# A two-layer interleaved attention kernel on one NeuronCore: the scheduler's planned times for DMA issue and landing, cross-engine waits, layer norm and softmax are changed

## The chip, the cores and the metric

One core of a Trainium2 chip runs the kernel. The metric is device time in microseconds (us), the median of the runs. Five engines work side by side, each through its own list of instructions in order: TensorE (PE, with its weight loads shown apart as PEld), VectorE (DVE), ScalarE (ACT), GpSimd (POOL) and SyncE (SP). SP issues the DMAs spoken of here. An instruction that has to wait holds back everything behind it on its engine.

## The reference

Four residual layers work on 2048 positions of width 576. Layers 1 and 3 ("A") are a dilated local attention; layers 2 and 4 ("B") are a recurrent attention over 64 segments of 32 positions, where each segment also sees 8 memory rows that the segment before left.

```python
def _A_ref(x, wqkv, wo):                   # H = 32 heads of 18, W = 8 keys, every 2nd position
    qkv = (x @ wqkv) ...                   # [3, H, S, 18]
    kg, vg = k[:, :, idx_c], v[:, :, idx_c]          # keys pos, pos-2, .. pos-14
    attn = softmax(where(mask, q . kg * 18 ** -0.5, -1e9))
    return (attn . vg) @ wo

def _B_ref(x, mem0, Wq, Wk, Wv, Wo, seg_len):        # 32 heads of 128
    mem = mem0                                       # 8 rows
    for s in range(n_seg):
        h = concatenate([mem, x[s * 32:(s + 1) * 32]])
        q, k, v = h Wq, h Wk, h Wv
        p = softmax(where(mask, q k^T * 128 ** -0.5, -1e9))
        o = (p v) Wo
        mem, out_s = o[:8], o[8:]

x = x + _A_ref(_layernorm(x), A_wqkv, A_wo)
x = x + _B_ref(_layernorm(x), B_mem0, ...)
x = x + _A_ref(_layernorm(x), A_wqkv, A_wo)
x = x + _B_ref(_layernorm(x), B_mem0, ...)
```

## The kernel before

The program runs 70 steps. In step t, `b_step` takes segment t of layer 2 and segment t-6 of layer 4 together: 80 columns in the tile `hT`, of which 16 are memory. It does the query and key products (`qk`, eleven groups of three heads, L728 and L730), the value products (`vpass`, L759), the scores with a softmax (`scores`, `softmax`), the products with the values (`pv_m` for the memory rows, L817; `pv_x` for the others, L850), and the output projection (`oproj`, L874). The memory rows of the output go straight into the next step's `hT`.

Every second step a tile of 64 positions of layer 1 and one of layer 3 (`a_tile`) go through beside this: load, layer norm, the three projections (L479), the key products on POOL, the logits on PE (L528), a softmax, the probabilities spread back over rows by PE in two parts (L552: 16 matmuls, then 4), the products with the values on DVE, a tree of three additions (tile `big`, then `oT`), the output projection (L587), and a second layer norm whose result goes out to HBM as `xn2T` or `xn4T`. From there `load_x` fetches it into a step's `hT` (L704).

The weights of the A layers do not stay on the chip's inner memory. They lie in HBM as 20 blocks, and each tile fetches all 20 again, one DMA per block (`wblock`, L423), into a ring of six buffers named `ring`. That makes 1280 loads. A block's five matmuls free its buffer for the next load.

PE writes into PSUM. Three tiles `r` there serve nearly everything (`qk`, `vpass`, `scores`, the layer norms' sums, the projections). One large tile `o` (pool `o4`) serves the spreading and both products with the values in turn. The next writer of such a tile waits until ACT or DVE has carried the last contents out.

What sets the order is a planner. Each piece of work is an operation with an engine, a planned length `us`, a priority, the operations it depends on and the buffers it takes (`_Plan.op`). `_Plan.run` plays the program with those lengths: when an engine comes free it takes the ready operation with the lowest priority number whose buffers are free, and at that moment the operation's instructions are written into the engine's list. A result counts as there `LAT` after the operation's end, or `lat` where that is given. Where an operation may run on either of two engines, the one that is free first in the plan takes it. So a planned time changes no instruction; it changes the order in which each engine gets them, and which of two engines gets some. On the chip the real waits are held by semaphores.

```python
                        if all(len(self.pools[p]) >= k for p, k in need.items()):
                            pick = o
                            break
...
                    heapq.heappush(events, (free[e] + (self.LAT[e] if o.lat is None else o.lat), n, ("done", o)))
```

Of the kernel before, what the change touches and what calls it, by code (L numbers as in the profile page):

```python
# [10 lines left out]
ACT = mybir.ActivationFunctionType  # L11
# [14 lines left out]
D = 576  # L26
T = 64
NS = T // SEG
# [27 lines left out]
class _Plan:  # L56
# [2 lines left out]

    LAT = {"PE": 0.22, "DVE": 0.1, "ACT": 0.1, "POOL": 0.12, "SP": 2.4, "NONE": 0.0}
    SWITCH = 0.1

    def __init__(self):
# [129 lines left out]
class _K:  # L195
# [190 lines left out]
    def layernorm(self, xT, dep, prio, writer, wus, wacq=(), wuses=()):  # L386

        nc, pl = self.nc, self.pl
        xs, st, ps = pl.buf("xs"), pl.buf("st"), pl.buf("r")
        a = pl.op(AD_, (0.46, 0.49), lambda e: self.copy(e, xs.t[:, :, 0, :], xT.t[:]), prio, [dep], acq=[xs], uses=[xT])  # L390

        def square(e):
            if e == "ACT":
                nc.scalar.activation(out=xs.t[:, :, 1, :], in_=xT.t[:], func=ACT.Square)
# [9 lines left out]
        c = pl.op("PE", 0.29, mm, prio, [b], acq=[ps], uses=[xs])  # L404

        def stats(e):
            m, r = st.t[:, 0, :], st.t[:, 1, :]
            nc.vector.tensor_scalar(out=m, in0=ps.t[:, 0:T], scalar1=1.0 / D, scalar2=None, op0=ALU.mult)
            nc.vector.tensor_tensor(out=r, in0=m, in1=m, op=ALU.mult)
            nc.vector.scalar_tensor_tensor(out=r, in0=ps.t[:, T:2 * T], scalar=1.0 / D, in1=r, op0=ALU.mult, op1=ALU.subtract)  # L410
        d = pl.op("DVE", 0.8, stats, prio, [c], acq=[st], uses=[ps])

        def rstd(e):
            r = st.t[:, 1, :]
            nc.scalar.activation(out=r, in_=r, func=ACT.Ln, bias=self.epsb[:, 0:1], scale=1.0)
            nc.scalar.activation(out=r, in_=r, func=ACT.Exp, scale=-0.5)
        f = pl.op("ACT", 0.6, rstd, prio, [d], uses=[st])
        return pl.op("POOL", wus, lambda e: writer(e, st.t[:, 0, :], st.t[:, 1, :]), prio, [f], acq=wacq,
                     uses=[st, xT, *wuses])

    def wblock(self, i, prio, dep):
        w = self.pl.buf("ring")
        o = self.pl.op("SP", 0.4, lambda e: self.nc.sync.dma_start(out=w.t[:], in_=self.wA[i]), prio, [dep], acq=[w], lat=2.7)  # L423
        return w, o

    def a_tile(self, layer, j, dep, due, span):
# [4 lines left out]
        def pr(f):  # L431
            return due - span * (1.0 - f)
        xT = pl.buf("xT")
        if layer == 1:
            x0, ps = pl.buf("x0"), pl.buf("r")
            a = pl.op("SP", 0.4, lambda e: nc.sync.dma_start(out=x0.t[0:T, 0:D], in_=self.A_x[0, j * T:(j + 1) * T, :]),
                      pr(0), [dep], acq=[x0])

            def tr(e, ps=ps):
# [6 lines left out]
        else:  # L446
            dl = pl.buf("dl")

            def ld(e):
                nc.sync.dma_start(out=xT.t[:], in_=self.x1T[:, j])  # L450
                nc.sync.dma_start(out=dl.t[:], in_=self.dT[0][:, NS * j:NS * j + NS])
            a = pl.op("SP", 0.8, ld, pr(0), [dep, self.x1_stored[j], *self.d_stored[0][NS * j:NS * j + NS]], acq=[xT, dl])

            def add(e):
                xv = xT.t[:].rearrange("p c (s n) -> p c s n", n=SEG)
# [111 lines left out]
                   pr(0.6), [b], uses=[ps, big])  # L567
        mus = []
        for c0, nb in ((0, 2), (2, 2), (4, 1)):
            mus.append(pl.op("DVE", 0.15 + 0.27 * nb,  # L570
                             lambda e, c0=c0, nb=nb: self.tt(e, big.t[:, c0:c0 + nb], big.t[:, c0:c0 + nb], win(vT.t, c0, nb), ALU.mult),
                             pr(0.62), evs + [got[2], got[2, "h"]] if nb == 2 else [e4, got[2], got[2, "h"]], uses=[big, vT]))
        oT = pl.buf("oT")
# [19 lines left out]
        xst = pl.op("SP", 0.4, lambda e: nc.sync.dma_start(out=(self.x1T if layer == 1 else self.x3T)[:, j], in_=xT.t[:]),  # L593
                    pr(0.95), [o], uses=[xT])
        (self.x1_stored if layer == 1 else self.x3_stored)[j] = xst
        xnb = pl.buf("xnb")
# [1 line left out]
        def wr2(e, m, rstd):  # L598
# [12 lines left out]
        o = pl.op("SP", 0.4, lambda e: nc.sync.dma_start(out=self.xnT[lane][:, NS * j:NS * j + NS], in_=xnb.t[:]),  # L611
                  pr(0.95), [o], uses=[xnb])
        self.xn_stored[lane][j] = o

    def finish_out(self, j, prio):
# [6 lines left out]
        a = pl.op("SP", 0.8, ld, prio, [self.x3_stored[j], *self.d_stored[1][NS * j:NS * j + NS]], acq=[xT, dl])  # L622
# [6 lines left out]
        for n, (c0, c1) in enumerate(((0, 4), (4, 5))):  # L629
# [8 lines left out]
            def ev(e, n=n, ps=ps):  # L638
# [6 lines left out]
        pl.op("SP", 0.4, lambda e: nc.sync.dma_start(out=self.out[0, j * T:(j + 1) * T, :], in_=ot.t[0:T, :]), prio, [o],  # L645
              uses=[ot])


# [6 lines left out]
    def softmax(self, ps, e_, n, prio, dep, mul, view, eview, last, pt, ptpool):  # L655
# [20 lines left out]
        def norm(e):  # L676
# [4 lines left out]
            nc.vector.reciprocal(out=s, in_=s)  # L681
            if mul == "DVE":
                nc.vector.tensor_tensor(out=v, in0=v, in1=s.unsqueeze(len(shp) - 1).to_broadcast(shp), op=ALU.mult)
# [11 lines left out]
    def load_x(self, t):  # L695

        nc, pl = self.nc, self.pl
        hT = pl.buf("hT")
        self.hT[t] = hT
        segs = [(l, self.lane_seg(t, l)) for l in range(2) if self.lane_seg(t, l) is not None]  # L700

        def ld(e):
            for l, s in segs:
                nc.sync.dma_start(out=hT.t[:, :, XC[l]:XC[l] + SEG], in_=self.xnT[l][:, s])  # L704
        o = pl.op("SP", 0.4 * len(segs), ld, t - 0.42, [self.xn_stored[l][s // NS] for l, s in segs] + [self.qk_op.get(t - 1)],
                  acq=[hT])
# [192 lines left out]
    def x_out(self, t, dep, prio):  # L899
# [8 lines left out]
        for lane in range(2):  # L908
            s = self.lane_seg(t, lane)
            if s is not None:  # L910
                self.d_stored[lane][s] = pl.op("SP", 0.4, lambda e, lane=lane, s=s: nc.sync.dma_start(out=self.dT[lane][:, s], in_=st.t[:, lane]),
                                               prio, [o], uses=[st])

    def b_step(self, t):
# [123 lines left out]
```

## Time and profile before

| what | value |
|---|---|
| median of 3 runs | 2835.91 us (2834.46 to 2848.84) |
| profiled execution, its own time | 2859.22 us |
| span of that execution | 2857.4 us |
| PE busy | 2451.8 us, 86% |
| DVE, ACT, POOL busy | 1839.1, 977.9 and 882.5 us |
| mean granted TensorE clock | 0.960 |
| DMA moved | 304.10 MB, mean 106 GB/s |

The profile page gives busy times, a chain of work that ended last, and groups of instructions. The view of waits lists who waited for whom: total us, number of times, the longest. The view of windows gives each engine's busy time in chosen stretches with the granted clock. The timeline lists instructions in order of time; its number in brackets is the engine's idle time just before, with what ended it. The profiled execution took 23.3 us more than the median of the runs; one sum below is made against the profiled time and then carried over.

### The profile page before, as it was taken

To read this page: it belongs to the slowest core of one execution; us is meant where nothing else is said; L and a number is where in the kernel's file an instruction comes from. 1 tells how busy PE (TensorE), PEld (TensorE's weight loads), DVE (VectorE), ACT (ScalarE), POOL (GpSimd) and SP (SyncE) were. 2 spreads that over 40 slices of the span, in tenths; PEclk is the share of its full clock that TensorE was granted. 3 is DMA by queue.
4 is the path that set the end of the run, shared out by engine and by line. 5 is a ranking of instruction groups with operands and counts; after the bars stand their busy time and mean duration, and the time that the engine had idled before them with its cause. 6 is when DMAs were issued, how large, how long until landed. Compare 5 with 4: busy or idle time off the path is not lost.

```text
span 2857.4 us, 159357 instructions
## 1 busy us (share of the span) xinstructions
PE 2451.8 (86%) x73360; PEld 2021.4 (71%) x73360; DVE 1839.1 (64%) x3981; ACT 977.9 (34%) x2165; POOL 882.5 (31%) x1122
## 2 busy tenths in 40 slices
PE   0289999888898998888898989889889898999998
PEld 0177777777777776777777777777777777777777
DVE  1266777666666676666766667666666666766665
ACT  0023333333333333333433333333333333332222
POOL 3321333233333333323333333333333333321110
PEclk9999999999999999999999999999999999999999
DMA  7622344333434434333434433433343443332210
GB/s 264 185 60 71 102 111 121 100 95 105 113 112 121 115 99 115 103 91 105 119 109 118 122 107 105 117 107 94 105 114 109 118 121 110 100 87 74 79 34 18
DMA packets 368644, 304.10 MB, mean 106 GB/s; under 512 B 146788, under 2 KB 364452, under 8 KB 366436
## 3 DMA queue, kind: packets, MB, share of 16 engines
q1 hardware_dynamic: 364724, 275.02, 34.5%
q0 software_dynamic: 3248, 18.88, 1.8%
q8 instruction: 573, 9.39, 1.4%
q14 instruction: 99, 0.81, 0.1%
HBM read 260.88 MB, written 32.90 MB: 103 GB/s over the span
## 4 chain that ended last, share of the span: by engine, by line
PE 58%; DVE 15%; DMA 10%; ACT 9%; issue 4%; SPq 3%; POOL 1%; ACTq 0%; DVEq 0%; POOLq 0%
PE r L728 17%; PE psY L874 14%; PE r L759 12%; DMA ring<-wA_blk 10%; PE r L479 5%; PE r L730 4%; DVE big L230 4%; ACT big L223 3%; DVE big L225 2%; SPq L300 2%; DVE OT L225 2%; ACT OT L223 2%; PE o L817 2%; PE o L850 1%; DVE r L671 1%
## 5 line engine op out<-in xcount | busy, mean ns | idle before, releaser
L728 PE MATMUL r<-hT,wq 128*128 128x80 bf16 x8960 | 695.0, 202 | 31.3 <-DVE V L225 17.3
L728 PE MATMUL r<-hT,wk 128*128 128x80 bf16 x8960 | 694.1, 202 | 0.0
L728 PEld LDWEIGHTS <-wq 128*128 128x128 bf16 x8960 | 468.1, 100 | 86.5 <-issue 79.3
L759 PE MATMUL r<-wv,hT 128*32 128x512 bf16 x6720 | 481.2, 408 | 12.9 <-ACT em L673 3.4
L874 PE MATMUL psY<-OT,wo 128*128 128x80 bf16 (+1 forms) x11360 | 474.7, 210 | 17.4 <-issue 9.3
L225 DVE CAST qk<-r 128x480 bf16<-128x480 f32 (+1 forms) x465 | 294.1, 632 | 299.3 <-PE r L730 295.1
L874 PEld LDWEIGHTS <-wo 128*128 128x128 bf16 x11360 | 457.3, 105 | 23.7 <-issue 22.1
L728 PEld LDWEIGHTS <-wk 128*128 128x128 bf16 x8960 | 465.4, 100 | 0.0
L730 PE MATMUL r<-hT,wq_r 128*128 128x80 bf16 x2240 | 452.6, 202 | 1.8 <-issue 1.8
L730 PE MATMUL r<-hT,wk_r 128*128 128x80 bf16 x2240 | 452.9, 202 | 0.0
L230 POOL TENSOR_TENSOR big<-qT,kT 128x1024 bf16<-128x1024 bf16 (+1 forms) x192 | 329.0, 1722 | 152.6 <-ACT kT L223 143.9
L759 PEld LDWEIGHTS <-hT 128*32 128x32 bf16 x8400 | 214.9, 101 | 224.8 <-issue 77.3
L479 PE MATMUL r<-xn,ring 128*128 128x64 bf16 x4800 | 236.2, 198 | 99.1 <-DMA ring<-wA_blk 83.1
L230 POOL TENSOR_TENSOR ex<-ex,sum 128x384 bf16<-128x384 bf16 x140 | 124.1, 886 | 603.8 <-DVE sum L681 383.0
L479 PEld LDWEIGHTS <-ring 128*128 128x128 bf16 x4800 | 179.0, 100 | 162.4 <-DMA ring<-wA_blk 108.9
L223 ACT ACTIVATE qk<-r 128x480 bf16<-128x480 f32 x305 | 170.4, 570 | 241.9 <-PE r L730 238.3
L730 PEld LDWEIGHTS <-wq_r 128*128 128x128 bf16 x2240 | 224.1, 100 | 1.9 <-issue 1.9
L223 ACT ACTIVATE V<-r 128x512 bf16<-128x512 f32 x265 | 158.2, 597 | 195.4 <-PE r L759 193.1
L730 PEld LDWEIGHTS <-wk_r 128*128 128x128 bf16 x2240 | 224.3, 100 | 0.0
L225 DVE CAST OT<-o 128x512 bf16<-128x512 f32 x138 | 95.2, 691 | 161.3 <-ACT OT L223 76.8
L223 ACT ACTIVATE OT<-o 128x256 bf16<-128x256 f32 (+1 forms) x282 | 131.1, 490 | 165.2 <-DVE OT L225 97.4
L759 PE MATMUL r<-wv_r,hT 128*32 128x512 bf16 x1680 | 178.6, 405 | 1.7 <-issue 1.7
(137 smaller groups left out, 3561.3 us busy)
## 6 DMA issues: line engine op xcount, KB each, us to landing
ring<-wA_blk SPq DMA_DIRECT2D x1280, 160.0 KB, 3.1
x1T<-xT SPq DMA_DIRECT2D x32, 160.0 KB, 1.8
d2T<-stg SPq DMA_DIRECT2D x64, 80.0 KB, 2.4
xT<-x1T SPq DMA_DIRECT2D x32, 160.0 KB, 2.3
dl<-d2T SPq DMA_DIRECT2D x32, 160.0 KB, 2.6
x3T<-xT SPq DMA_DIRECT2D x32, 160.0 KB, 3.2
d4T<-stg SPq DMA_DIRECT2D x64, 80.0 KB, 3.1
xT<-x3T SPq DMA_DIRECT2D x32, 160.0 KB, 3.4
```

The source lines that it names most:

```text
L223: nc.scalar.activation(out=out, in_=in_, func=ACT.Copy, scale=1.0 if scale is None else scale)
L225: (nc.vector if e == "DVE" else nc.gpsimd).tensor_copy(out=out, in_=in_)
L230: (self.nc.vector if e == "DVE" else self.nc.gpsimd).tensor_tensor(out=out, in0=in0, in1=in1, op=op)
L300: nc.sync.dma_start(out=self.wA[i], in_=wn[:, :, col0:col0 + P])
L479: nc.tensor.matmul(ps.t[:, c * T:(c + 1) * T], lhsT=w.t[:, kc, :], rhs=xn.t[:, kc, :], start=(kc == 0), stop=(kc == 4))
L671: nc.vector.tensor_tensor(out=v, in0=v, in1=m.unsqueeze(len(shp) - 1).to_broadcast(shp), op=ALU.add)
L728: nc.tensor.matmul(pv[:, hh, wi, :], lhsT=wt[:, kc, h * P:(h + 1) * P], rhs=hT.t[:, kc, 0:W80], start=(kc == 0), stop=False)
L730: nc.tensor.matmul(pv[:, hh, wi, :], lhsT=wr[:, (h % 16) * P:(h % 16 + 1) * P], rhs=hT.t[:, 4 + h // 16, 0:W80], start=False, stop=True)
L759: nc.tensor.matmul(ps.t[c * 32:(c + 1) * 32, :], lhsT=l, rhs=w, start=(kc == 0), stop=(kc == 4))
L817: nc.tensor.matmul(ps.t[:, c, i * 16:(i + 1) * 16], lhsT=V[b].t[q4, r, i, :], rhs=pt.t[q4, i, b, 0:16], start=(i == 0 and b == 0), stop=(i ...
L850: nc.tensor.matmul(o, lhsT=V[b].t[q4, r, i, :], rhs=p, start=(r == 0 and i == 0 and b == 0), stop=(r == 1 and i == 3 and b == 2), skip_gro ...
L874: nc.tensor.matmul(psY.t[:, mb, c0:], lhsT=self.wo[:, w0:w0 + P], rhs=self.OT[:, h, c0:], start=(h == 0 and mb == 0), stop=(h == NH - 1 an ...
```

## The change

Only planned numbers change. A DMA issue on SP goes from 0.4 to 0.5 us, its landing from 2.4 to 2.8 us, and that of a ring block from 2.7 to 3.2 us. The hop from DVE and ACT to others goes from 0.1 to 0.08 us, and from POOL from 0.12 to 0.08. Of the chains, the layer norm's statistics go from 0.8 to 0.98 us, the writing of its result for a B layer from 2.0 to 2.1, its matmuls from 0.29 to 0.28, the reciprocal part of a softmax from 0.05 to 0.06 over its 0.65, and a product with the values from 0.27 to 0.3 a block.

```diff
-    LAT = {"PE": 0.22, "DVE": 0.1, "ACT": 0.1, "POOL": 0.12, "SP": 2.4, "NONE": 0.0}
+    LAT = {"PE": 0.22, "DVE": 0.08, "ACT": 0.08, "POOL": 0.08, "SP": 2.8, "NONE": 0.0}
...
-        d = pl.op("DVE", 0.8, stats, prio, [c], acq=[st], uses=[ps])
+        d = pl.op("DVE", 0.98, stats, prio, [c], acq=[st], uses=[ps])
...
-        o = self.pl.op("SP", 0.4, lambda e: self.nc.sync.dma_start(out=w.t[:], in_=self.wA[i]), prio, [dep], acq=[w], lat=2.7)
+        o = self.pl.op("SP", 0.5, lambda e: self.nc.sync.dma_start(out=w.t[:], in_=self.wA[i]), prio, [dep], acq=[w], lat=3.2)
...
-            mus.append(pl.op("DVE", 0.15 + 0.27 * nb,
+            mus.append(pl.op("DVE", 0.15 + 0.3 * nb,
...
-        o = self.layernorm(xT, o, pr(0.8), wr2, 2.0, wacq=[xnb])
+        o = self.layernorm(xT, o, pr(0.8), wr2, 2.1, wacq=[xnb])
...
-        o = pl.op("DVE", 0.65 + (0.6 if mul == "DVE" else 0.05), norm, prio, [o], acq=[ss], uses=[e_])
+        o = pl.op("DVE", 0.65 + (0.6 if mul == "DVE" else 0.06), norm, prio, [o], acq=[ss], uses=[e_])
```

The other lines of the diff give the remaining SP operations (`x`, `x1T`, `x3T`, `xn2T`, `xn4T`, `hT`, `d2T`, `d4T`, `out`) 0.5 instead of 0.4 a DMA.

The lists of all five engines come out in another order. Three places are shown, all from the steady middle of the program.

The program repeats every two steps. On SP, in the second step of such a pair, the store of a layer-3 tile's normed result (`xn4T`) and the load that reads it back into `hT` stood, before:

```order
L611 DMA xn2T<-xnb_325 128x384
L423 DMA ring_336<-wA_blk 128x640
L620 DMA xT_303<-x3T 128x320
L621 DMA dl_305<-d4T 128x320
L423 DMA ring_335<-wA_blk 128x640
L423 DMA ring_331<-wA_blk 128x640
L611 DMA xn4T<-xnb_324 128x384
L423 DMA ring_332<-wA_blk 128x640
L704 DMA hT_264<-xn2T 128x6x32
L704 DMA hT_264<-xn4T 128x6x32
L423 DMA ring_333<-wA_blk 128x640
```

and stand now:

```order
L423 DMA ring_332<-wA_blk 128x640
L611 DMA xn4T<-xnb_324 128x384
L423 DMA ring_335<-wA_blk 128x640
L620 DMA xT_303<-x3T 128x320
L621 DMA dl_305<-d4T 128x320
L423 DMA ring_336<-wA_blk 128x640
L423 DMA ring_331<-wA_blk 128x640
L423 DMA ring_334<-wA_blk 128x640
L704 DMA hT_264<-xn2T 128x6x32
L704 DMA hT_264<-xn4T 128x6x32
```

Between the store and the loads of `hT` there are now six other DMAs, four of them ring blocks, where there was one.

On PE, a little later in the same step, the layer-3 projection (L479) has just had two ring blocks after the scores. Before, two more blocks followed at once (the first two rows end the second block):

```order
L479 LDWEIGHTS ring_334
L479 MATMUL r_340<-xn_310,ring_334 128x64
L479 LDWEIGHTS ring_336
L479 MATMUL r_340<-xn_310,ring_336 128x64
L479 LDWEIGHTS ring_336
```

and now the value products follow (`hT` is their weight there):

```order
L479 LDWEIGHTS ring_332
L479 MATMUL r_341<-xn_310,ring_332 128x64
L759 LDWEIGHTS hT_265
L759 MATMUL r_340<-wv,hT_265 32x512
L759 LDWEIGHTS hT_265
```

The blocks of that projection are spread among other work, and the value products take `r_340`, the tile that the scores of the memory rows have just used.

On POOL, in the first step of a pair, the tail of one A tile (`big`, `oT`) and the key products of the other (`big<-qT,kT`) stood, before:

```order
L505 COPY halo_317<-vT_313 128x70
L230 TENSOR_TENSOR oT_323<-big_319 128x320
L230 TENSOR_TENSOR big_319<-qT_311,kT_312 128x1024 x2
L230 TENSOR_TENSOR ex_272<-ex_272,sum_299 128x8x48
L230 TENSOR_TENSOR big_319<-qT_311,kT_312 128x512
```

and stand now:

```order
L505 COPY halo_317<-vT_313 128x70
L230 TENSOR_TENSOR big_319<-big_319 128x5x256
L230 TENSOR_TENSOR big_319<-big_319 128x5x128
L230 TENSOR_TENSOR oT_323<-big_319 128x320
L230 TENSOR_TENSOR big_319<-qT_311,kT_312 128x1024
L230 TENSOR_TENSOR ex_272<-ex_272,sum_299 128x8x48
L230 TENSOR_TENSOR big_319<-qT_311,kT_312 128x1024
L230 TENSOR_TENSOR big_319<-qT_311,kT_312 128x512
```

The two large additions of that tree were on DVE and are on POOL now, and the normalising of a softmax (`ex`) has come between the key products. Over the whole program POOL does 58 of the 64 first additions instead of 29, and 26 of the second instead of none.

More of the change, by code (lines that the diff above doesn't have):

```diff
@@ L403, in mm @@
                                  rhs=xs.t[:, c].rearrange("p a t -> p (a t)"), start=(c == 0), stop=(c == 4))
-        c = pl.op("PE", 0.29, mm, prio, [b], acq=[ps], uses=[xs])
+        c = pl.op("PE", 0.28, mm, prio, [b], acq=[ps], uses=[xs])
         def stats(e):
@@ L435, in a_tile @@
             x0, ps = pl.buf("x0"), pl.buf("r")
-            a = pl.op("SP", 0.4, lambda e: nc.sync.dma_start(out=x0.t[0:T, 0:D], in_=self.A_x[0, j * T:(j + 1) * T, :]),
+            a = pl.op("SP", 0.5, lambda e: nc.sync.dma_start(out=x0.t[0:T, 0:D], in_=self.A_x[0, j * T:(j + 1) * T, :]),
                       pr(0), [dep], acq=[x0])
@@ L451, in ld @@
                 nc.sync.dma_start(out=dl.t[:], in_=self.dT[0][:, NS * j:NS * j + NS])
[L452 removed]
+            a = pl.op("SP", 1.0, ld, pr(0), [dep, self.x1_stored[j], *self.d_stored[0][NS * j:NS * j + NS]], acq=[xT, dl])
             def add(e):
@@ L592, in a_tile @@
                   pr(0.75), [o], uses=[ps, xT])
-        xst = pl.op("SP", 0.4, lambda e: nc.sync.dma_start(out=(self.x1T if layer == 1 else self.x3T)[:, j], in_=xT.t[:]),
+        xst = pl.op("SP", 0.5, lambda e: nc.sync.dma_start(out=(self.x1T if layer == 1 else self.x3T)[:, j], in_=xT.t[:]),
                     pr(0.95), [o], uses=[xT])
@@ L610, in a_tile @@
         lane = 0 if layer == 1 else 1
-        o = pl.op("SP", 0.4, lambda e: nc.sync.dma_start(out=self.xnT[lane][:, NS * j:NS * j + NS], in_=xnb.t[:]),
+        o = pl.op("SP", 0.5, lambda e: nc.sync.dma_start(out=self.xnT[lane][:, NS * j:NS * j + NS], in_=xnb.t[:]),
                   pr(0.95), [o], uses=[xnb])
@@ L621, in ld @@
             nc.sync.dma_start(out=dl.t[:], in_=self.dT[1][:, NS * j:NS * j + NS])
-        a = pl.op("SP", 0.8, ld, prio, [self.x3_stored[j], *self.d_stored[1][NS * j:NS * j + NS]], acq=[xT, dl])
+        a = pl.op("SP", 1.0, ld, prio, [self.x3_stored[j], *self.d_stored[1][NS * j:NS * j + NS]], acq=[xT, dl])
         def add(e):
@@ L644, in finish_out @@
             o = a2
-        pl.op("SP", 0.4, lambda e: nc.sync.dma_start(out=self.out[0, j * T:(j + 1) * T, :], in_=ot.t[0:T, :]), prio, [o],
+        pl.op("SP", 0.5, lambda e: nc.sync.dma_start(out=self.out[0, j * T:(j + 1) * T, :], in_=ot.t[0:T, :]), prio, [o],
               uses=[ot])
@@ L704, in ld @@
                 nc.sync.dma_start(out=hT.t[:, :, XC[l]:XC[l] + SEG], in_=self.xnT[l][:, s])
-        o = pl.op("SP", 0.4 * len(segs), ld, t - 0.42, [self.xn_stored[l][s // NS] for l, s in segs] + [self.qk_op.get(t - 1)],
+        o = pl.op("SP", 0.5 * len(segs), ld, t - 0.42, [self.xn_stored[l][s // NS] for l, s in segs] + [self.qk_op.get(t - 1)],
                   acq=[hT])
@@ L910, in x_out @@
             if s is not None:
-                self.d_stored[lane][s] = pl.op("SP", 0.4, lambda e, lane=lane, s=s: nc.sync.dma_start(out=self.dT[lane][:, s], in_=st.t[:, lane]),
+                self.d_stored[lane][s] = pl.op("SP", 0.5, lambda e, lane=lane, s=s: nc.sync.dma_start(out=self.dT[lane][:, s], in_=st.t[:, lane]),
                                                prio, [o], uses=[st])
```

## The prediction

> **What bounds the kernel now.** I read the page first, then who waits for whom, the granted clock, and the stretches around the largest waits.
>
> ```profile
> PE 2451.8 (86%) x73360; PEld 2021.4 (71%) x73360; DVE 1839.1 (64%) x3981; ACT 977.9 (34%) x2165; POOL 882.5 (31%) x1122
> ...
> PE 58%; DVE 15%; DMA 10%; ACT 9%; issue 4%; SPq 3%; POOL 1%; ACTq 0%; DVEq 0%; POOLq 0%
> ```
>
> PE bounds: it is busy 86% of the span and holds 58% of the chain that ended last. The same 73,360 matmuls run after the change, so what can move is the 405.6 us in which PE is not busy (the span of 2857.4, in a row below, less 2451.8), and the pace at which it works. From the view of waits, PE's part:
>
> ```profile
> PEld L479 <- DMA ring<-wA_blk: 108.9, 148, 3.0
> PE r L441 <- DMA x<-in_A_x_dram: 103.2, 1, 103.2
> PE r L479 <- DMA ring<-wA_blk: 83.1, 85, 2.9
> PE o L817 <- ACT big L223: 24.3, 29, 1.4
> PE o L552 <- ACT big L223: 23.8, 27, 1.1
> PE o L552 <- DVE big L225: 18.9, 32, 2.7
> PE r L728 <- DVE V L225: 17.3, 35, 0.7
> PE o L817 <- ACT OT L223: 13.8, 26, 0.5
> PE r L728 <- ACT qk L223: 9.9, 26, 0.4
> PE r L528 <- POOL big L230: 3.6, 2, 2.6
> ```
>
> The 103.2 us are the start of the program; the edit does not reach them. Of the rest the ring blocks are the largest: 83.1 us of idle PE, 108.9 us as the weight loads see the same waits. I take 100, between them, since a matmul is still shown busy for a while after the next could have begun. Then come the two parts of the spreading (L552) and the first product with the values (L817), which wait for the one tile `o`. The pace:
>
> ```profile
> core 0: 2857.4 us, clock 0.960
> ```
>
> A mean of 0.960 means that 0.040 x 2857 = 114 us of PE's work were lost to a lower clock. Where, windows of 3.4 us around the two largest clumps of waits show (width, PE busy, clock, DMA share, GB/s):
>
> ```profile
> 1500.20:1503.60 3.40, 1.63 (x77) 1.00 0.54 152
> 1503.60:1507.00 3.40, 2.93 (x86) 0.50 0.39 115
> 1507.00:1510.40 3.40, 3.40 (x98) 1.00 0.15 53
> ...
> 1524.10:1527.50 3.40, 3.14 (x96) 1.00 0.85 249
> 1527.50:1530.90 3.40, 1.62 (x56) 1.00 0.73 204
> 1530.90:1534.30 3.40, 3.40 (x37) 0.50 0.54 118
> ```
>
> A window in which PE was busy for 1.6 us is followed by one at half clock; the window after one with 3.14 or 2.93 us busy has the full clock. A half-clock window costs 1.7 us, so 114 us are about 67 of them, two in each of the 35 pairs of steps. One belongs to the spread and one to the ring:
>
> ```profile
> 1498.99 0.40 PE L552 MATMUL o<-e,epadT 32*128 32x128 bf16 x16
> ...
> 1500.23 0.89 PE L587 MATMUL r<-oT,ring 128*128 128x64 bf16 x25
> 1502.02 0.24 PE L552 MATMUL o<-e,epadT 32*128 32x128 bf16 x4 [0.90 <-ACT big L223]
> 1503.04 0.51 PE L817 MATMUL o<-ptm,V 32*128 32x16 bf16 x48 [0.78 <-ACT big L223]
> 1504.07 0.53 PE L817 MATMUL o<-ptm,V 32*128 32x16 bf16 x48 [0.53 <-ACT OT L223]
> ```
>
> ```profile
> 1526.99 0.32 PE L800 MATMUL r<-qk 128*32 128x80 bf16 x16
> ...
> 1527.95 0.32 PE L479 MATMUL r<-xn,ring 128*128 128x64 bf16 x5
> 1528.99 0.32 PE L479 MATMUL r<-xn,ring 128*128 128x64 bf16 x5 [0.72 <-DMA ring<-wA_blk]
> 1530.27 0.74 PE L479 MATMUL r<-xn,ring 128*128 128x64 bf16 x10 [0.96 <-DMA ring<-wA_blk]
> ```
>
> **The change part by part.** No instruction is added or dropped; the sum is over waits that the new orders move.
>
> *Ring blocks.* A reload needs its issue and its landing:
>
> ```profile
> L423 SPq DMA_DIRECT2D ring<-wA_blk x1280: 314/382/2109, 104.2 to 2719.9; - x183
> ring<-wA_blk SPq DMA_DIRECT2D x1280, 160.0 KB, 3.1
> ```
>
> That is 0.38 + 3.1 = 3.5 us and a little for the hand-over, nearly 4. In PE's order I counted, for each of the 1274 reuses of a buffer, the matmuls between the last of one block and the first of the next, at about 35 ns each (98 in 3.40 us at full clock, quoted above) and the value products at their own pace. Under 4 us of such cover lay 368 reuses before and lie 206 now, 56%; under 3.75 us 241 and 146, 61%. If the waits shrink in that measure, 0.42 x 100 = 42 us go. SP's order helps (the load of `hT` from `xn4T` now has six DMAs ahead of it in place of one):
>
> ```profile
> SPq L704 <- DMA xn4T<-xnb: 66.2, 30, 4.0
> ```
>
> These 66.2 us held back the ring blocks queued behind. Against it, the store of `xn2T` now stands ahead of the five ring blocks that it used to follow, and if the layer norm is late, they are late. Bounds: 0 (SP blocked elsewhere) to 100 (no ring wait left). I take -42.
>
> *The two spreads of a pair of steps.* Between the two parts of the first one 60 query and key matmuls stood, 2.1 us; now stand 135, 4.7 us. Its wait, the row for DVE `big`, 18.9 us, goes except for the few tiles at the ends: -14 (bounds 0 and -19). In the second spread the scores, a load and the output projection stood between, 66 matmuls in 1.7 us, and 0.90 us were waited; now stand 25 matmuls, 1.2 us at their pace. What is awaited is four copies out of `o`:
>
> ```profile
> L223 ACT ACTIVATE big<-o 128x512 bf16<-128x512 f32 x221 | 125.9, 597 | 154.1 <-PE o L552 110.8 <-DVE big L225 37.0
> ```
>
> Three stand on ACT and one on DVE: 3 x 0.60 and a hop, about 2 us, so a wait of 0.8 as before; if they take 2.6 us as at 1499.4 to 1502.0, it is 1.4. For 25 spreads -2 to +12; I take +5. The two halves of the first product with the values no longer stand together: -14 (the row ACT `OT`, 13.8). The output projection then waits for the second half's copy, some 0.35 us behind a layer norm's sums: +9 for 26 tiles (0 to +14).
>
> *PSUM tiles.* Reuses of `r` after a query and key group with less than 1.3 us between fall from 217 to 144 and after value products from 139 to 87, about two thirds. The rows of L728 hold 27.2 us for these: -8 (0 to -27). But the value products now follow the scores' tile after 0.92 us, where its release takes
>
> ```profile
> L670 DVE TENSOR_REDUCE nmx<-r 128x4 f32<-128x320 f32 x140 | 68.0, 486 | 4.0 <-PE r L800 3.8
> L671 DVE TENSOR_TENSOR r<-r,nmx 128x320 f32<-128x320 f32 x140 | 69.9, 499 | 4.8
> L673 ACT ACTIVATE em<-r 128x320 bf16<-128x320 f32 x140 | 61.0, 436 | 144.9 <-DVE r L671 129.5 <-PE r L479 15.4
> ```
>
> 0.49 + 0.50 + 0.44 = 1.43 us: 0.5 us or more, 28 times, is 14 us or more, unless a ring wait covers it. +8 (0 to +25).
>
> *The tree on POOL.* Durations now and then:
>
> ```profile
> L230 POOL TENSOR_TENSOR big<-big 128x1280 bf16<-128x1280 bf16 x29 | 75.6, 2608 | 12.2 <-DVE big L230 12.2
> L230 DVE TENSOR_TENSOR big<-big 128x640 bf16<-128x640 bf16 x64 | 32.7, 512 | 46.0 <-POOL big L230 44.8
> L230 DVE TENSOR_TENSOR big<-big 128x1280 bf16<-128x1280 bf16 x35 | 28.9, 825 | 1.2
> L230 POOL TENSOR_TENSOR ex<-ex,sum 128x384 bf16<-128x384 bf16 x140 | 124.1, 886 | 603.8 <-DVE sum L681 383.0 <-ACT xs L394 220.8
> ```
>
> The first addition costs 2.61 - 0.83 = 1.78 us more; the second, on POOL, is not in the trace: 1280 elements take 2.61 there, half of that or somewhat more makes 1.4, 0.9 over DVE's 0.51 (bounds 0.8 and 2.1). With `ex` (0.89) in between, the key products end 3.6 us later against the spread. PE's logits, which await them, have moved back behind some 3 us more of PE work (12.9 after the spread's second part, 9.8 before); the cover is nearly whole. The logits' wait, 3.6 us in all in the row of L528, rises by 0 to 28; I take +8. Without that cover it would be 3.6 x 26 = 94.
>
> *The clock.* If the ring's clump shrinks from 1.7 us of wait to about 1, most of its windows at half clock go: 35 x 1.7 = 60 us at most, I take 25 windows, -40. The spread's clump adds up as before (0.8 + 0.8 + 0.35 against 0.90 + 0.78 + 0.53) and keeps its windows. Bounds 0 and -75.
>
> In the Trainium skill, "TensorE: Matmul & The Clock Gate", Part 1 on the clock gate, the half clock follows an idle window of about 3.4 us. The width agrees with these rows, but here 1.6 us of work within a window did not prevent it. By that rule as it stands no wait of this kernel (3.0 us at the longest) reaches the gate and the change would gain nothing by the clock: the rival "clock stays", below.
>
> The sum: -42 - 14 + 5 - 14 + 9 - 8 + 8 + 8 - 40 = -88 us. 2859.2 - 88 = 2771 for an execution like the profiled one, which took 23.3 us more than the median; 2835.9 - 88 = 2748, and **I predict 2750 us**.
>
> **Rivals.** *The clock stays.* As many windows fall below what keeps the clock up, because 1 us of ring wait and the new wait behind the scores lie close together. Then -48: 2788. For it: only two clumps are shown, with nothing between 1.6 and 2.9 us busy. Against it: the scattered waits elsewhere left the clock at 1.00.
>
> *The waits change places.* Landing is later where DMA is dense (share 0.85 in the window before the ring's clump), SP's other entries block the ring as before, and what ring and spread give is taken by the scores' tile and the logits: -42 + 42, only the PSUM and spread gains of some 10 are left: 2825 to 2836.
>
> *Slower: the tree on POOL decides.* The key products end later than PE reaches the logits; PE stands, 26 times, behind a matmul that cannot go, and gains a half-clock window each. The break-even is at 88 / 26 = 3.4 us a pair, or 1.7 us with its half-clock window; from there the kernel is slower. At 2.5 + 1.7 us it is +109 - 88 = +21: 2857. For it: POOL gets about 110 us more work, and a DVE multiplication of 0.49 us took up to 1.92 beside POOL's work, so both may stretch:
>
> ```profile
> L683 DVE TENSOR_TENSOR em<-em,sum x140: 491/493/1924, 162.0 to 2835.0; 128x320 bf16<-128x320 bf16 x140
> ```
>
> Against it: the logits moved back too, and they hardly waited before.
>
> **How the numbers follow.** Forecast 0.56, own range 2705 to 2780; the clock stays 0.20; waits change places 0.11; slower 0.13. The range that leaves out 2 in 10 runs from 2695 (most of the ring's and the clock's bounds) to 2845. A measurement here can tell 0.5%, 14 us, from no change: faster 0.77 (forecast, clock stays, and the lower edge of the third), same 0.10, slower 0.13.
>
> **What would show it.** Right: the ring's rows at L479 fall from 83.1 and 108.9 to about 50 and 63; the granted clock rises from 0.960 to about 0.975; L552 behind DVE `big` nearly vanishes; SP's wait at L704 shrinks; new rows appear for L759 behind ACT `em`. Wrong: ring rows as before (the cover count does not carry), a clock of 0.960 with shorter waits, or L528 behind POOL `big` with some 60 us or more.

## The result, and the profile after

The changed kernel takes 2744.91 us (median of 4 runs, 2743.75 to 2747.74) where the kernel before takes 2835.18 us in the same comparison: a ratio of 0.968, with a 95% interval from 0.964 to 0.972. The forecast was 2750 us.

The profiled execution after took 2747.74 us, the one before 2859.22: 111.5 us less. The page's first part and the view of cores of the changed kernel:

```profile
PE 2388.5 (87%) x73360; PEld 2001.8 (73%) x73360; DVE 1927.1 (70%) x4021; ACT 936.5 (34%) x2070; POOL 980.0 (36%) x1177
```

```profile
core 0: 2745.9 us, clock 0.980
```

PE does the same 73,360 matmuls. It is busy 63.3 us less (2451.8 to 2388.5), and it stands idle 48.2 us less (405.6 to 2745.9 - 2388.5 = 357.4). The two make up the difference of the spans. The first is the clock: 0.020 x 2746 = 55 us are lost to it now, 114 were before. The second is waits. PE's part of the view of waits after:

```profile
PEld L479 <- DMA ring<-wA_blk: 76.1, 110, 2.2
...
PE r L479 <- DMA ring<-wA_blk: 50.5, 70, 2.1
PE o L552 <- ACT big L223: 39.1, 28, 1.5
PE o L817 <- ACT big L223: 21.5, 29, 0.8
PE r L759 <- ACT em L673: 21.1, 57, 0.9
PE r L759 <- DVE st L410: 18.1, 28, 0.7
PE o L850 <- issue: 13.8, 17, 1.8
PE psY L874 <- ACT OT L223: 9.4, 11, 1.8
...
PE o L552 <- DVE big L225: 6.4, 6, 2.8
PE r L728 <- DVE V L225: 6.2, 15, 0.4
...
PE r L528 <- POOL big L230: 3.6, 2, 2.6
```

and the rows of before for those of these lines that the forecast did not show:

```profile
PE o L850 <- issue: 26.1, 21, 2.2
...
PE psY L874 <- issue: 9.3, 25, 0.6
...
PE psY L874 <- ACT OT L223: 6.7, 10, 1.0
...
PE r L759 <- ACT em L673: 3.4, 12, 0.9
...
PE r L759 <- DVE st L410: 1.6, 3, 0.5
```

The ring's wait fell by a third (83.1 to 50.5, 108.9 to 76.1 as the weight loads see it). The first spread's went (L552 behind DVE `big`), and the second's grew (L552 behind ACT `big`). The value products (L759) wait much longer in two places, behind ACT `em` and DVE `st`, 34 us more in all. Two rows of SP's part of the view after:

```profile
SPq L911 <- ACT stg L223: 327.6, 38, 30.3
...
SPq L704 <- DMA xn4T<-xnb: 5.3, 5, 2.4
```

The second row was 66.2 before. The first is new in this size (104.8 before): SP stands up to 30 us at a store (of `stg`, L911) with all its later DMAs queued behind, and yet the ring's wait on PE fell.

### The profile page after: what moved, and what is told of

The parts are those of the page before. It is cut to its first block, busy times and chain, and to the rows that moved or that the text cites. A ratio compares the mean times of both kernels' runs of the same rounds, so it can differ in the third digit from the quotient of the medians.

```text
span 2745.9 us, 159278 instructions
## 1 busy us (share of the span) xinstructions
PE 2388.5 (87%) x73360; PEld 2001.8 (73%) x73360; DVE 1927.1 (70%) x4021; ACT 936.5 (34%) x2070; POOL 980.0 (36%) x1177
## 5 line engine op out<-in xcount | busy, mean ns | idle before, releaser
L728 PE MATMUL r<-hT,wq 128*128 128x80 bf16 x8960 | 694.5, 202 | 11.5 <-DVE V L225 6.2
L728 PE MATMUL r<-hT,wk 128*128 128x80 bf16 x8960 | 693.9, 202 | 0.0
L728 PEld LDWEIGHTS <-wq 128*128 128x128 bf16 x8960 | 463.8, 100 | 48.7 <-issue 45.2
L874 PE MATMUL psY<-OT,wo 128*128 128x80 bf16 (+1 forms) x11360 | 482.4, 208 | 18.7 <-ACT OT L223 9.4
L225 DVE CAST qk<-r 128x480 bf16<-128x480 f32 (+1 forms) x506 | 324.4, 642 | 242.2 <-PE r L730 219.6
L759 PE MATMUL r<-wv,hT 128*32 128x512 bf16 x6720 | 447.3, 384 | 51.6 <-ACT em L673 21.1
L874 PEld LDWEIGHTS <-wo 128*128 128x128 bf16 x11360 | 460.2, 104 | 30.3 <-issue 23.9
L728 PEld LDWEIGHTS <-wk 128*128 128x128 bf16 x8960 | 465.3, 100 | 0.1
L759 PEld LDWEIGHTS <-hT 128*32 128x32 bf16 x8400 | 208.9, 97 | 229.8 <-issue 73.4
L230 POOL TENSOR_TENSOR ex<-ex,sum 128x384 bf16<-128x384 bf16 x140 | 117.0, 836 | 536.1 <-DVE sum L681 482.5
L479 PE MATMUL r<-xn,ring 128*128 128x64 bf16 x4800 | 235.3, 196 | 62.5 <-DMA ring<-wA_blk 50.5
L479 PEld LDWEIGHTS <-ring 128*128 128x128 bf16 x4800 | 179.7, 99 | 123.1 <-DMA ring<-wA_blk 76.1
L230 POOL TENSOR_TENSOR big<-big 128x1280 bf16<-128x1280 bf16 (+1 forms) x84 | 187.5, 2232 | 130.5 <-DVE big L230 128.5
L223 ACT ACTIVATE qk<-r 128x480 bf16<-128x480 f32 (+1 forms) x264 | 146.7, 558 | 204.0 <-PE r L730 197.0
L223 ACT ACTIVATE OT<-o 128x512 bf16<-128x512 f32 (+1 forms) x299 | 143.1, 500 | 154.7 <-DVE OT L225 92.2
L223 ACT ACTIVATE big<-o 128x512 bf16<-128x512 f32 x220 | 125.1, 596 | 168.1 <-PE o L552 112.8
```

Of the source, the lines that this page charges most:

```text
L223: nc.scalar.activation(out=out, in_=in_, func=ACT.Copy, scale=1.0 if scale is None else scale)
L225: (nc.vector if e == "DVE" else nc.gpsimd).tensor_copy(out=out, in_=in_)
L230: (self.nc.vector if e == "DVE" else self.nc.gpsimd).tensor_tensor(out=out, in0=in0, in1=in1, op=op)
L479: nc.tensor.matmul(ps.t[:, c * T:(c + 1) * T], lhsT=w.t[:, kc, :], rhs=xn.t[:, kc, :], start=(kc == 0), stop=(kc == 4))
L728: nc.tensor.matmul(pv[:, hh, wi, :], lhsT=wt[:, kc, h * P:(h + 1) * P], rhs=hT.t[:, kc, 0:W80], start=(kc == 0), stop=False)
L759: nc.tensor.matmul(ps.t[c * 32:(c + 1) * 32, :], lhsT=l, rhs=w, start=(kc == 0), stop=(kc == 4))
```

## The experiments

Each kernel is timed beside the kernel before, whose medians in the three groups of runs were 2839.84 us (the halves, the ring alone, the seventh buffer), 2836.50 (issue and landing apart, 2.2, 4.0) and 2835.19 (the rest). "Plan" is the planned issue plus landing of a ring block; waits, idle and clock are those of the profiled execution.

| kernel | plan, us | ring wait PE / PEld, us | PE idle / busy, us | clock | median, us | ratio to before (95%) |
|---|---|---|---|---|---|---|
| before | 3.1 | 83.1 / 108.9 | 405.6 / 2451.8 | 0.960 | 2835 to 2840 | 1 |
| after | 3.7 | 50.5 / 76.1 | 357.4 / 2388.5 | 0.980 | 2744.91 | 0.968 (0.964 to 0.972) |
| SP's numbers only | 3.7 | 24.4 / 41.3 | 350.3 / 2398.3 | 0.977 | 2750.26 | 0.965 (0.962 to 0.969) |
| all others only | 3.1 | 101.1 / 133.0 | 398.5 / 2450.7 | 0.960 | 2846.27 | 1.001 (0.998 to 1.003) |
| ring block only | 3.7 | 39.1 / 59.9 | 361.7 / 2408.6 | 0.972 | 2776.46 | 0.976 (0.972 to 0.980) |
| ring's issue only | 3.2 | 63.5 / 91.8 | 377.2 / 2414.1 | 0.970 | 2814.94 | 0.991 (0.988 to 0.994) |
| ring's landing only | 3.6 | 51.5 / 77.8 | 377.7 / 2412.4 | 0.971 | 2797.79 | 0.987 (0.983 to 0.990) |
| landing 2.2 | 2.6 | 110.4 / 154.3 | 411.1 / 2454.3 | 0.960 | 2868.13 | 1.012 (1.009 to 1.014) |
| before, 7th buffer | 3.1 | 66.2 / 91.1 | 393.8 / 2431.7 | 0.966 | 2830.82 | 0.995 (0.993 to 0.998) |
| before, useless matmuls | 3.1 | 74.2 / 100.3 | 388.3 / 2507.8 | 0.963 | 2886.84 | 1.019 (1.015 to 1.024) |
| SP's, landing 4.0 | 4.5 | 8.7 / 18.3 | 316.3 / 2360.7 | 0.991 | 2677.32 | 0.944 (0.942 to 0.945) |
| that, other DMAs 3.4 | 4.5 | 11.1 / 23.9 | 308.6 / 2356.3 | 0.992 | 2663.97 | 0.940 (0.936 to 0.944) |
| SP's, landing 4.8 | 5.3 | 4.6 / 7.8 | 295.0 / 2360.1 | 0.990 | 2659.26 | 0.938 (0.935 to 0.942) |
| whole change, landing 4.0 | 4.5 | 18.1 / 33.1 | 364.5 / 2387.4 | 0.977 | 2748.93 | 0.970 (0.967 to 0.974) |

For the ring's issue or landing alone the profiled execution was the fastest of its six and of its four (2793.09 and 2791.77 us), so its waits are on the low side of what the median stands for.

### Which half: SP's numbers, the others, the ring block alone

SP's numbers only: the nine SP operations and `"SP": 2.8` of the diff.

```diff
-    LAT = {"PE": 0.22, "DVE": 0.1, "ACT": 0.1, "POOL": 0.12, "SP": 2.4, "NONE": 0.0}
+    LAT = {"PE": 0.22, "DVE": 0.1, "ACT": 0.1, "POOL": 0.12, "SP": 2.8, "NONE": 0.0}
...
+        o = self.pl.op("SP", 0.5, ... lat=3.2)
```

> Only the planned times of SP's operations are changed (issue 0.5, landing 2.8, ring block 3.2); hops, layer norm, softmax and value products are planned as before. In PE's order the two spreads of a pair of steps stand as before the change (60 and 66 matmuls between their parts), while the ring's covers are as long as with the whole change or longer. Theory A (ring waits and the half-clock windows behind them carry the gain): most of it is here, 2765 us (2745 to 2790), L479 behind the ring at 50 us or less on PE, granted clock about 0.975, L552 behind DVE big still near 19 us. Rival B (the spreads and PSUM tiles, moved by the compute chains' times, carry it): 2810 us or more, clock near 0.965.

All others only:

```diff
+    LAT = {"PE": 0.22, "DVE": 0.08, "ACT": 0.08, "POOL": 0.08, "SP": 2.4, "NONE": 0.0}
...
+        c = pl.op("PE", 0.28, mm, ...)
+        d = pl.op("DVE", 0.98, stats, ...)
...
+            mus.append(pl.op("DVE", 0.15 + 0.3 * nb,
...
+        o = self.layernorm(xT, o, pr(0.8), wr2, 2.1, wacq=[xnb])
...
+        o = pl.op("DVE", 0.65 + (0.6 if mul == "DVE" else 0.06), norm, ...)
```

> The other half: hops, layer norm, softmax and value products planned with the new times, every SP operation as before. The spreads are as far apart as with the whole change or farther (155 and 25 matmuls), the ring's covers as short as before. Theory A: 2820 us (2800 to 2840), ring rows of L479 at 80 to 110 us, clock near 0.960. Rival B: 2770 us or less. If both halves bring less than a third each of the 90 us, the two act only together.

The ring block alone:

```diff
-        o = self.pl.op("SP", 0.4, ... lat=2.7)
+        o = self.pl.op("SP", 0.5, ... lat=3.2)
```

> One line of the diff alone: the ring block is planned with 0.5 us of issue and 3.2 of landing. Theory A: like the SP half, within 15 us of it, about 2770 us, with ring rows at half of before. Rival (the landings of the other transfers and SP's order around them matter as much): no better than 2815 us, with SP's wait at L704 behind xn4T still near 66 us.

SP's numbers alone give the whole gain (0.965), as theory A had it. The others alone give none (1.001), less than the 2820 us that was expected of them. The ring block's line alone gives about two thirds (0.976); it is 26 us behind SP's numbers, more than the 15 of its theory A, so SP's other numbers add to the gain. PE's part of the waits with SP's numbers only:

```profile
PE r L479 <- DMA ring<-wA_blk: 24.4, 32, 2.0
PE o L817 <- ACT big L223: 24.3, 29, 1.4
PE o L552 <- ACT big L223: 24.0, 27, 1.3
...
PE o L552 <- DVE big L225: 18.3, 31, 2.5
```

The three rows of the spreads stand as they stood before (24.3, 23.8, 18.9), and only the ring's has moved, by 58.7 us. With the clock (0.977 on a span of 2748.6: 63 us lost, 51 fewer) that is 110 us, and its span is 108.8 us shorter. So the ring and the clock account for the gain of this half. In the windows just ahead of stretches at half clock PE stood 56.5 us behind ring blocks before, and 3.3 us here.

The other half does what the forecast said of spreads and tiles, and makes the ring worse. Rows of its waits, of PE and then of SP:

```profile
PE r L479 <- DMA ring<-wA_blk: 101.1, 126, 2.9
PE o L552 <- ACT big L223: 37.5, 25, 1.5
...
PE o L552 <- DVE big L225: 8.7, 9, 2.8
```

```profile
SPq L704 <- DMA xn4T<-xnb: 28.6, 30, 4.0
```

The last row bears on a reason of the forecast. SP's wait at L704 more than halved here (66.2 to 28.6) while the ring's rose. So SP's wait there is not, by itself, what the ring's hangs on.

### A dose: the ring's issue and landing apart, and a landing that is too short

The same line as above with 0.5 and 2.7 (issue only), 0.4 and 3.2 (landing only), 0.4 and 2.2.

> The kernel before with the ring block's planned issue at 0.5 us and its landing still at 2.7. In most of the ring waits of before the buffer had been free for over 0.3 us when SP came to the load (73 of the 95 waits over 0.5 us), so SP's own pace could be what the plan had wrong. Theory 'issue': most of the ring line's 63 us are here, 2790 us, ring rows on PE near 45 us. Theory 'landing': 2828 us, ring rows near 75.

> The kernel before with the ring block's planned landing at 3.2 us and its issue still at 0.4. Theory 'landing': 2790 us, ring rows on PE near 45 us. Theory 'issue': 2825 us. By the count of reuses under 4 us of cover (368 before, 307 with the issue alone, 222 with the landing alone, 104 with both) the landing carries about twice what the issue does: 2800 against 2822.

> The wrong way: the kernel before with the ring block's planned landing at 2.2 us. Theory A (the plan's error at the ring sets the waits): slower, 2875 us (2850 to 2900), ring rows on PE above 105 us, clock at 0.955 or less; 483 reuses lie under 4 us of cover against 368. Rival 'any new order is as good as another, and the change was a lucky one': no relation to the direction, within 20 us of before either way.

```diff
+        o = self.pl.op("SP", 0.4, ... lat=2.2)
```

Issue alone gives 0.9%, landing alone 1.3%, both 2.4%. Neither of the two theories, that one number holds nearly all of it, came true; the estimate from the count (2800 against 2822 us) did roughly. The shorter landing makes the kernel slower by 1.2%, as theory A had it, though its clock stayed at 0.960 where 0.955 or less was expected. Over the kernels without the other half, with the six buffers of before and without added matmuls, the ring's wait falls with the column "plan", from 110.4 us at 2.6 to 4.6 at 5.3, and the time with it, through whichever number the plan was changed. A re-ordering that is good by chance would hardly follow a dose like that; it is the planned time that does it. (From 3.7 to 4.5 only a part of the gain is the ring's own, as shown below.)

### Is it the buffer? The kernel before with a seventh that the plan does not know

The program keeps the order of before; each ring buffer is reused one block later.

```diff
-                        if all(len(self.pools[p]) >= k for p, k in need.items()):
+                        if all(len(self.pools[p]) - (1 if p == "ring" else 0) >= k for p, k in need.items()):
...
-        tiles("ring", 6, [P, 5, P])
+        tiles("ring", 7, [P, 5, P])
```

> The kernel before in its own order on every engine, with a seventh ring buffer that the plan does not know of: each load may start about one block earlier, nothing else moves. This takes away part of the ring's waits and nothing else. Theory A: ring rows on PE fall from 83 to 50 us or less, the clock rises to 0.970 or more, and the time falls by more than the waits alone, to 2780 us (2755 to 2805). Rival (the blocks are late because SP is held back by other entries, or because landing takes 4 us where DMA is dense, not because a buffer is missing): ring rows above 70 us, 2825 us or more. Rival 'clock stays': the waits fall but the time only by as much, and the clock stays at 0.960.

The forecast's count, reuses with less than 4 us of matmuls between, falls from 368 to 185 by this, about as far as by the change itself (206). The time falls by 0.5% only, into the rival's 2825 us or more, though the ring's wait fell below the rival's 70 us. These are its waits for the ring:

```profile
PEld L479 <- DMA ring<-wA_blk: 91.1, 124, 2.9
...
PE r L479 <- DMA ring<-wA_blk: 66.2, 71, 2.8
```

The ring's wait falls by 17 us, half of what the change took from it. So the cover of a reuse decides a part at most. I then followed, in the trace of before, each of the 95 ring waits of over 0.5 us back to its load. In 73 of them (90 of 112 us) the buffer had been free for more than 0.3 us when SP came to the load; with the seventh buffer in 74 of 78. For these loads an earlier buffer would not have helped, since SP came to them later still.

What kept them, the trace of before tells in two parts. SP came late by 1.1 us (the median of the late ones), and for 74 of the 86 us of lateness in all it was issuing other DMAs: two or three in most cases, ring blocks above all, then the loads of L620 and L621 and the stores of L611; only one was a load of L704. And the transfers were slow: where the trace has the landing of such a load (39 of them), its median is 4.3 us, against 3.1 over all. The plan's 0.4 and 2.7 us were short of both. Coming late is not enough by itself, since SP came more than 0.3 us after the buffer to two in three of all the loads from 150 us on.

### Useless matmuls in the kernel before

To part waiting from the clock, 8, 24 and 8 matmuls of 128 columns were put ahead of the second to fourth block of layer 3's value projection, which was taken for the place of the ring's clump in the forecast's windows. They write columns of PSUM that nobody reads. Lines below move by 5.

```diff
+                fill = {1: 8, 2: 24, 3: 8}.get(c, 0) if layer == 3 and part == 2 else 0
...
+                    for _ in range(fill):
+                        nc.tensor.matmul(ps.t[:, 3 * P:4 * P], lhsT=self.ones[:, :], rhs=self.ident[:, :], ...)
```

> The kernel before, same order everywhere, with useless matmuls of 128 columns put just ahead of three blocks of the layer-3 value projection (8, 24 and 8 of them, ahead of blocks 1, 2 and 3), into columns of the PSUM tile that nobody reads: 40 x 0.056 = 2.2 us of PE work per tile, 72 us in all, at the place where 76 of the ring's waits stand (2.4 us a tile). The work fits into waits, so by itself it costs 0 to 20 us. Theory 'idle PE drops the clock': PE is now busy while it would have waited, the half-clock windows behind this clump go (some 25, 1.7 us each), the clock rises to 0.970 or more and the kernel gets faster by doing more: 2805 us (2785 to 2825). Rival 'the clock has to do with something else': clock 0.960, time 2835 to 2860.

It became slower by 1.9%, outside both theories, and the added matmuls stood in the wrong place. The windows at such a clump (columns as in the forecast's), and its timeline:

```profile
1535.70:1539.10 3.40, 3.19 (x115) 1.00 0.68 209
1539.10:1542.50 3.40, 1.05 (x20) 1.00 0.80 225
1542.50:1545.90 3.40, 3.40 (x37) 0.50 0.61 124
```

```profile
1538.78 0.32 PE L484 MATMUL r<-xn,ring 128*128 128x64 bf16 x5
1539.87 0.32 PE L484 MATMUL r<-xn,ring 128*128 128x64 bf16 x5 [0.77 <-DMA ring<-wA_blk]
1541.16 0.32 PE L484 MATMUL r<-xn,ring 128*128 128x64 bf16 x5 [0.98 <-DMA ring<-wA_blk]
```

No filler (L481) stands between these blocks: the clump belongs to the value projection of layer 1, and the filler stands in layer 3's alone. The part on the change calls the projection at this place layer 3's; it is layer 1's, and layer 3's comes some 20 us later, where PE hardly waits for the ring. The added work, 56 us of PE's busy time, went into the time almost in full (+52), and the clump kept its half clock. Whether work in the gap would hold the clock up, this run does not tell.

### A landing planned longer still, and the other half on top of it

Landing of a ring block 4.0 in SP's numbers only:

```diff
-        o = self.pl.op("SP", 0.5, ... lat=3.2)
+        o = self.pl.op("SP", 0.5, ... lat=4.0)
```

> The SP half of the change, with the ring block's planned landing raised further to 4.0 us, about what blocks take where DMA is dense. 41 reuses lie under 4 us of cover against 128. Theory A: ring rows on PE at 12 us or less (24 with 3.2), 2730 us (2710 to 2745), so it beats both kernels. Rival (blocks planned later than needed push other work out of place): ring rows shrink but other waits grow by as much, 2745 to 2765.

It gained 5.6%, more than was expected (2677 us against 2730). The ring's wait is nearly gone, and so are the rows of PE's waits that stood for the second spread, which has nothing to do with the ring:

```profile
PE r L479 <- DMA ring<-wA_blk: 8.7, 13, 1.7
...
PE o L817 <- ACT big L223: 4.5, 4, 1.4
...
PE o L552 <- ACT big L223: 1.3, 3, 0.6
```

L552 behind ACT `big` stood at 24.0 with SP's numbers only, and L817 behind it at 24.3. The timeline of its second spread shows why:

```profile
1488.59 0.40 PE L552 MATMUL o<-e,epadT 32*128 32x128 bf16 x16
1488.92 1.70 PE L874 MATMUL psY<-OT,wo 128*128 128x80 bf16 x40
1490.46 0.46 PE L587 MATMUL r<-oT,ring 128*128 128x64 bf16 x10
1490.75 0.88 PE L874 MATMUL psY<-OT,wo 128*128 128x80 bf16 x20
1491.59 0.24 PE L552 MATMUL o<-e,epadT 32*128 32x128 bf16 x4
...
1492.87 0.51 PE L817 MATMUL o<-ptm,V 32*128 32x16 bf16 x48
```

Here 2.7 us of work, 70 matmuls, stand between the two parts, and the copies out of `o` are done when PE gets there. (Its two parts start 3.0 us apart, as after's do at 1522.12 and 1525.12 below; but there 1.50 us of that was a wait.) Blocks that are planned later leave other work to go first, and here it went where it was needed. Against SP's numbers only, these two rows of the spread fell by 42.5 us and the ring's by 15.7, while other rows grew; so most of this step's gain in waits is not the ring's own. That it follows from the ring's number as a rule is not shown.

Landing 4.8, and 4.0 with the other DMAs' landing at 3.4 in place of 2.8:

> The SP half with the ring block's planned landing at 4.8 us, one step beyond 4.0 (2677 us). 27 reuses lie under 4.5 us of cover against 99. Theory A: the ring has only 9 us of waits left to give, so this is at best 10 us faster, 2670; blocks planned later than needed may cost more: 2665 to 2700. Theory 'the later the better without end': below 2650.

> The SP half with the ring block's landing at 4.0 us and that of all other transfers at 3.4 instead of 2.8 us (traces show 1.8 to 3.9). Theory A: SP's 20 us at L704 behind the store of xn4T shrink below 8 us, but no ring block waits behind them any more, so the time stays at 2677 within 12 us. Rival (other landings matter as the ring's did): 2655 us or less.

They took 2659.26 and 2663.97 us. Both lie between their two theories: the first gained more than the ring's last waits could give, the second 13 us, just beyond the 12 that theory A allowed. The intervals of these two and of the 4.0 alone touch, so which of the three is best stays open. The first beats the changed kernel by 3% (0.938 / 0.968 = 0.969).

The whole change, with the same 4.0:

> The whole change with the ring block's planned landing at 4.0 us. Theory A with the compute half worth nothing (as its own run showed): as the SP half with 4.0, 2677 us, give or take 15. Rival (with the ring's waits gone, the spreads and PSUM tiles show, and the compute half helps or hurts): off by more than 25 us either way.

It takes 2748.93 us, 72 us more than without the other half; the rival came true. The ring still waits little (18.1 us), but these rows of PE's waits are large:

```profile
PE o L817 <- ACT big L223: 29.9, 32, 1.0
PE o L552 <- ACT big L223: 20.5, 25, 0.8
...
PE r L759 <- ACT V L223: 18.1, 26, 0.7
...
PE r L479 <- ACT kT L223: 12.1, 23, 0.5
PE r L728 <- DVE qk L225: 11.6, 28, 0.4
```

The spread's waits are back, new waits for PSUM tiles have come, and the clock is 0.977 as against 0.991 (63 us lost in place of 24). Of the 75 us between the two spans, 48 are PE idle and 27 PE busy.

## Why the prediction was right, point by point

**What bounds, and where the gain came from: right.** PE's idle time and its clock carry the whole difference. The sum for idle time was -42 - 14 + 5 - 14 + 9 - 8 + 8 + 8 = -48, and 48.2 us went.

**The clock: right in mechanism, undersized.** It was put at 25 windows, -40; PE's busy time fell by 63.3 and the loss at a lower clock by 59. Counted in the records of the granted clock, stretches of 3.41 us at half clock fell from 68 to 33, so 35 windows went, each 1.7 us. In the windows just ahead of such stretches PE stood 56.5 us behind ring blocks before, and 3.7 now; the spread's waits there (L552 and L817 behind ACT `big`) were 37 us and are 40. So nearly all of the ring's windows went and the spread's stayed, as the forecast had it; the ring waits that are left hardly cost a window, where I had kept 10 of the 35. "The clock stays" fell with that. That the clock rises as the ring's wait falls is seen over the kernels of the table; where that wait grew (101.1 and 110.4 us), the clock stayed at 0.960. No run moved the clock at unchanged waits.

**The median was met partly by luck.** From profile to profile 111.5 us went, not 88: the undersized clock. The forecast carried 23.3 us over, by which the profiled execution before exceeded its median; after, the profiled execution is only 2.8 us over its median. The two errors cancel.

**The ring, -42: the right sign, -33 on both rows, but priced by the wrong measure.** The share of reuses with less than 4 us of cover, 56%, met the 61 and 70% of the wait that is left only roughly. The seventh buffer refutes it as the price: the same fall in that count took 17 us of the ring's wait in place of 33, and 0.5% of the time. The forecast had put a reload at "nearly 4" us from the moment that its buffer is free. In the waits that were followed back SP came 1.1 us after that, and issue and landing took 4.6 us more (medians). What stands in the count's place is when SP comes to a load, how slow that transfer is, and how far from its load the plan puts a block's matmuls; the dose shows that the planned issue and landing govern it. Which of the two lists, SP's or PE's, does more, no run tells, since one number moves both.

**SP's L704: right as a row (66.2 to 5.3), not shown as a help.** It fell in the half without the gain too, and with the landing at 4.0 it is 19.7 us where SP's numbers only had 5.8, though the ring waits less there.

**The spreads.** First one -14: 18.9 to 6.4, -12.5. Second one +5, with +12 as its bound: 23.8 to 39.1, +15.3. The forecast had named both lengths of the copies and chosen the shorter; most waits are now 1.50 us in place of 0.90, as with the longer. The row of ACT `OT`, -14: gone, 13.8 to nothing. The output projection behind the second half's copy, +9: 6.7 to 9.4, +2.7.

**PSUM tiles.** L728, -8 with -27 as its bound: the two rows fell from 27.2 to 6.2, -21. The value products behind the scores' tile, +8: 3.4 to 21.1, +17.7, within its 25. Not foreseen: they now also wait for the tile of a layer norm's sums (DVE `st`, 1.6 to 18.1, +16.5), and L850's and L874's stands without a cause that the profile shows shrank by 12.3 and 6.5. The sum of all this is as forecast only because these cancel.

**The tree on POOL, +8: nothing.** The logits wait 3.6 us behind POOL `big`, exactly as before, though POOL is busy 980.0 us instead of 882.5. The cover of PE's work was whole. The slower rival fell with it. "The waits change places" describes the compute half well, by itself 1.001, but not the ring.

**What the forecast did not say** is that its compute terms, -14 + 5 - 14 + 9 - 8 + 8 + 8 = -6, are a half of the change worth nothing, and that this half is a loss of 72 us once the ring's landing is planned at 4.0.

## What to carry to other kernels

In a kernel whose order comes out of planned times, the time that a DMA is planned to take is worth sweeping beyond the median that the trace shows: here a block lands in 3.1 us, and beside SP's other numbers a plan of 4.0 and 4.8 gave 1.6 and 1.8 times the gain of 3.2 (5.6 and 6.2% against 3.5), in part through work that came to stand better and that no rule here promises. One reason to look beyond the median is the spread: of the ring's landings that the trace of before has, one in ten took 4.3 us or more. Time each half of such a change apart, since here one half had the gain, and the other cost as soon as more of the gain was taken. A count of cover on the engine that waits says how a wait might move; before it is priced by it, follow some of the waits back to what the transfer's own issuer was doing.

## What the runs showed of the hardware

The half clock goes by windows on a fixed grid, so the same waits cost or don't by where they fall. In each of the traces all stretches at half clock but the first begin on a grid of 3.413 us, to within 0.01 of a window. In the changed kernel the second spread's two waits, 1.50 and 0.76 us, once fall across two windows and once nearly whole into one. The timeline of the changed kernel at both places, and then the windows, laid on that grid to within 0.03 us:

```profile
1522.12 0.40 PE L552 MATMUL o<-e,epadT 32*128 32x128 bf16 x16
...
1525.12 0.24 PE L552 MATMUL o<-e,epadT 32*128 32x128 bf16 x4 [1.50 <-ACT big L223]
1526.11 0.51 PE L817 MATMUL o<-ptm,V 32*128 32x16 bf16 x48 [0.76 <-ACT big L223]
...
1599.04 0.24 PE L552 MATMUL o<-e,epadT 32*128 32x128 bf16 x4 [1.50 <-ACT big L223]
1600.03 0.52 PE L817 MATMUL o<-ptm,V 32*128 32x16 bf16 x48 [0.76 <-ACT big L223]
```

```profile
1521.60:1525.00 3.40, 2.02 (x58) 1.00 0.76 235
1525.00:1528.40 3.40, 2.38 (x93) 1.00 0.17 60
...
1596.70:1600.10 3.40, 1.15 (x34) 1.00 0.72 229
1600.10:1603.50 3.40, 3.40 (x91) 0.50 0.01 4
```

With 2.02 and 2.38 us busy in the two windows the clock stays. With 1.15 us busy in one, the next has half clock. The Trainium skill, "TensorE: Matmul & The Clock Gate", Part 1 on the clock gate, has the window as free-running and 3413 ns long, and the traces agree in both. The condition that the Trainium skill gives there, an idle window of that length, is stricter than what they show, since 1.15 us of work within the window did not keep the clock up. So the same 2.26 us of waits cost another 1.7 us or nothing more, by where they fall.

Counted over the windows of that grid at full clock, from 150 us on, in before and after together: all 53 with less than 1.6 us of PE busy were followed by one at half clock, none of 1307 with more than 2.2 us was, and of the 74 between them 37 were. Between 110 and 150 us, at the start of PE's steady work, it is otherwise: nine windows with less than 1.6 us busy, one of them with 0.30 us, were followed by full clock. So the busy time of one window is not the whole rule, and what else belongs to it is not shown.
